# Another hand-written order for the opening of a fused window-attention and squared-ReLU kernel

## The chip, the core and the metric

The kernel runs on one core of a Trainium2 chip. The metric is device time in microseconds (us) of one execution, as the median of several runs. The core has five engines that run side by side and meet through semaphores: PE (matrix products, with PEld as its weight loads), DVE (vector), ACT (activation functions), POOL (GpSimd, which here also issues most of the loads) and SP (which issues the other loads and the stores). Each engine executes its own instructions strictly in the order in which the program issued them.

## The reference

Four batches of 768 tokens, 8 heads of 64. A token attends to the 128 latest tokens and to the first 4 ("sinks"). The attention output, 3072 x 512, goes through two dense layers with a squared ReLU between them.

```python
scores = scale * np.matmul(q, k.transpose(0, 1, 3, 2))
keep = is_sink | in_window            # 4 sinks, window of 128
a = softmax(np.where(keep, scores, -1e9))
x = (a @ v).transpose(0, 2, 1, 3).reshape(B * S, H * D)
h = x @ w_in                          # 512 -> 2048
r = np.maximum(h, 0.0)
out = (r * r) @ w_out                 # 2048 -> 512
```

## The kernel before

Everything is cut into some 990 small steps ("ops"), each of which is a function that issues one or a few instructions on one engine. The steps are built by loops over batches, groups and pairs of heads, and numbered in the order of building. They are then issued in the order of a long string, `ORDER`, written into the file. A word of it is a step's number, sometimes with a letter for the engine (`p` PE, `d` DVE, `a` ACT, `g` POOL; the first engine that the step allows otherwise) and with `+0` or `+1` for the PSUM pool that it takes a buffer from. PSUM is held as four buffers of two banks, two in a pool `den` and two in a pool `att`; SBUF scratch is handed out from pools of numbered buffers (`qr`, `qs`, `expm`, `r` and others) in the same way. A buffer is taken from the front of a list of free ones, so the order also settles which earlier step a later one has to wait for. `DUMMIES` says ahead of which steps `warm` issues passes of PE whose result is overwritten: 128x128 products with the identity, into the buffer that the step is about to fill.

```python
            o.engine = names[word[-1]] if word[-1] in names else next(iter(o.engines))
            for s in o.takes:
                if len(s.pools) > 1:
                    s.pool = s.pools[int(chosen.pop(0))]
                s.room = free[s.pool].pop(0)
            self.idle = DUMMIES.get(n, 0)
            o.run(o.engine)
```

Batch 0 is taken in three groups of 256 tokens. The first two groups are loaded as float32 with SP and ACT queues (steps 7 to 15), cast on DVE or ACT, turned on PE, copied out of PSUM, and so on; the third is loaded by POOL with a cast on the way (27 to 30). The steps that the prediction names are these:

| steps | what they do |
|---|---|
| 7, 9 / 8, 10 | load keys / queries of group 0, head pairs 0-1 and 2-3 |
| 12, 14 / 13, 15 | the same for group 1 |
| 19, 20, 22, 23, 31, 32 | load value tiles 0 to 5 (POOL) |
| 21, 24, 25, 26 / 33 to 36 | load the four quarters of the first / second weight matrix (POOL) |
| 27, 28 / 29, 30 | load keys / queries of group 2; 37 to 44 those of batch 1 |
| 991 | passes that warm PE up |
| 55, 60 / 56, 61 | cast keys / queries of group 0; 88, 93 / 89, 94 those of group 1 |
| 57, 62 | turn (transpose) group 0, pairs 0-1 and 2-3: the first two turns; 58, 59, 63, 64 copy them out |
| 90, 95 | the same for group 1; 91, 92, 96, 97 copy them out |
| 67, 68, 75, 76 | scores of group 0 (the mask is added by a product with `ident`); 69, 70, 77, 78 their exponentials |
| 71, 73, 79, 81 | weighted values of group 0; 72, 74, 80, 82 divide by the sums |
| 83, 85 | turn the attention output of group 0; 84, 86 copy it out |
| 100, 101, 110, 111 | scores of group 1; 102, 104, 112, 114 exponentials; 103, 105, 113, 115 masks |
| 66, 98, 99 | sink keys, sink scores, sink exponentials |
| 106, 108, 116, 118 | values of group 1; 107, 109, 117, 119 divide; 120 to 123 turn and copy out |
| 152 to 183 | first dense layer of groups 0 and 1: two PE steps, a ReLU and a square for each of 8 blocks |
| 124 to 151 | turn, scores, values of group 2 |
| 282 to 289 | second dense layer of group 0 |
| 331, 332, 334 / 278, 279 | sums of the first / second weight matrix, used later by products that save a multiplication |
| 184 | the PE step next after 289, the last word that the change touches |

All loads that POOL issues go through one queue, in the order of issue. From step 184 on the order is the same in both kernels, to the end of the program.

Of the kernel before, what the change touches and what calls it, by code (L numbers as in the profile page):

```python
# [18 lines left out]


ORDER = """
990 1 0 2 7 8 9 10 11 12 13 14 15 16 17 18 56a 991+0 55d 61a 3 60d 57+1 62+0 19 20 59a 5 6 58d 4 65 63d 67+0 21 64a
75+1 69 89d 22 77 23 76+0 68+0 24 25 70 71+1 88d 73 93d 90+0 78 79+1 72 94a 81 74 83+0 92d 100+1 91a 80 102 82 95+0 66
97d 26 85 110+1 101+1 96d 103g 104 84d 98+0 27 86d 152+0 105g 99 112 111+0 153 114 115g 106+1 113d 28 29 116+1 108
160+0 107 117 154a 30 109 118 119 161 120+1 121a 31 122 168+1 123d 169 32 33 34 155a 170a 162d 172+1 331 164+0 176+0
171d 163a 165 35 166d 36 167d 156+1 173 157 177 174d 124+1 158a 37 38 125a 126d 39 180+1 127+0 332 133+1 181 129d 178a
128a 136 130+1 179d 282+1 182d 334 131 141+1 132+0 140+1 183d 283 40 144 142 137g 284 285 41 145d 159d 143d 134 146+1
135d 147 286 138+1 287 288 278 139 42 43 148+0 175a 150 149d 151d 289 44 279 184+1 290 185 193+0 280 281 200+0 201 291
194 45 204+1 196+0 202 46 203 205 198a 186 197 207a 293 206 187+0 199a 216+0+0 47 48 195a 217 49 188d 234+1+0 50 235
190+0 219 208+0 87 292 237 209 295 191 218 297+0 189 220 51 336 52 212 53 210a 294 211 255+0 252+1 254 299 298 256 54  # L30
253a 257 444 223+0+1 333 238d 445 192a 226 304 213 224 221+0 312 222 300 241+1+0 301 214+0 296 244 215 302 225 446
# [26 lines left out]
985 967d 969 983 984 989 986 988 987  # L58
"""
DUMMIES = {  # L60
    57: 31, 62: 24, 75: 4, 85: 3, 110: 4, 991: 29,
}


# [1345 lines left out]
```

## Time and profile before

| | us |
|---|---|
| runs | 211.52, 211.09, 210.98; median 211.09 |
| the profiled execution's own time | 209.94 |
| its span, first to last instruction | 208.2 |
| PE busy | 200.9 (96%) |
| DVE busy | 178.0 (85%) |
| ACT busy | 131.6 (63%) |
| POOL busy | 98.6 (47%) |

In the rows that the prediction shows, a row of the timeline is: start, duration, engine, line of the program, operation, tile written <- tiles read, shape, how many in a row; in brackets the idle time ahead of it and what ended that. L503 is a turn, L609 and L602 are scores, L678 values, L727 the turn of the attention output, L762 the first dense layer, L990 the second dense layer of group 0, L185 and L1372 the passes that are thrown away; L192 and L194 are copies and casts on ACT and DVE, L630 an exponential, L642 and L218 masks on DVE and POOL, L694 and L695 the division, L776 and L778 the ReLU. A matmul's end is modelled and some 0.2 us after the next one starts, so the cost of a step on PE is read from one start to the next. A row of the windows has the window, its length, the busy time of PE, PEld, DVE, ACT and POOL in it, the granted clock of PE, and two numbers on the loads.

### The profile page before, as it was taken

The numbers are of one execution on the slowest core, as the hardware profiler recorded it, in microseconds if no ns is written. First come the engines' busy times: TensorE is split into PE (matmuls) and PEld (weight loads), VectorE is DVE, ScalarE is ACT, GpSimd is POOL, SyncE is SP. The second block draws the span as 40 slices with busy tenths as digits, with TensorE's granted clock in tenths as the row PEclk, the third lists the DMA queues.
The fourth block names the chain that finished last, engine by engine and source line by source line (L and its number), as shares of the span: only waits on it lengthen the run. The fifth ranks groups of instructions, "written<-read, shape, count | busy, mean of one in ns | idle before, by whom it ended". The sixth has DMA issues, their size and how long they took to land.

```text
span 208.2 us, 6087 instructions
## 1 busy us (share of the span) xinstructions
PE 200.9 (96%) x2535; PEld 177.6 (85%) x2535; DVE 178.0 (85%) x343; ACT 131.6 (63%) x205; POOL 98.6 (47%) x141
## 2 busy tenths in 40 slices
PE   7979999999899999999999999999999999999993
PEld 7757997579878889889878988998889999999893
DVE  5385767989999998999998888999989998998853
ACT  2678428718988168899888448989871452584010
POOL 7767983899489936989523529000280000000000
PEclk9999999999999999999999999999999999999999
DMA  5999999999999999999999995901023220200205
GB/s 162 218 216 202 184 186 213 177 155 179 148 61 118 156 137 241 92 188 154 129 138 229 108 136 152 159 0 25 4 50 127 57 82 22 101 0 3 99 5 201
DMA packets 96043, 26.12 MB, mean 125 GB/s; under 512 B 86800, under 2 KB 93456, under 8 KB 96016
## 3 DMA queue, kind: packets, MB, share of 16 engines
q0 software_dynamic: 69248, 12.59, 82.7%
q1 hardware_dynamic: 25568, 12.49, 28.6%
q10 hardware_dynamic: 1200, 0.66, 1.1%
q8 instruction: 20, 0.33, 0.6%
q14 instruction: 7, 0.06, 0.1%
HBM read 27.30 MB, written 6.29 MB: 161 GB/s over the span
## 4 chain that ended last, share of the span: by engine, by line
PE 76%; DVE 10%; DMA 6%; ACT 5%; issue 1%; ACTq 0%
PE py L1239 25%; PE pm L892 25%; PE pm L762 9%; DMA qr<-in_q_dram 6%; PE po L678 5%; PE ps L609 4%; PE py L990 3%; PE py L1100 2%; PE pt L503 1%; DVE sg L1213 1%; DVE xn_sb L695 1%; DVE r L942 1%; ACT gT_sb L915 1%; ACT qkT L192 1%; DVE gT_sb L1213 1%
## 5 line engine op out<-in xcount | busy, mean ns | idle before, releaser
L630 ACT ACTIVATE expm<-ps 128x1024 bf16<-128x1024 f32 (+1 forms) x48 | 44.1, 953 | 10.0 <-PE ps L609 8.9
L218 POOL TENSOR_SCALAR_AFFINE_SELECT expm<-expm 128x512 bf16<-128x512 bf16 x38 | 26.5, 730 | 46.9 <-ACT expm L630 21.5
L942 DVE CUSTOM_DVE_ANT_0 r<-pm,t 128x512 bf16<-128x512 f32 x54 | 36.0, 684 | 1.6 <-PE pm L892 1.2
L1239 PEld LDWEIGHTS <-gT_sb 128*128 128x128 bf16 x320 | 30.4, 98 | 4.5 <-issue 0.9
L892 PEld LDWEIGHTS <-w_in_sb 128*128 128x128 bf16 x384 | 32.5, 114 | 1.7 <-issue 1.5
L192 ACT ACTIVATE t<-pm 128x512 f32<-128x512 f32 x42 | 24.7, 600 | 13.4 <-PE pm L892 12.7
L192 ACT ACTIVATE osb<-py 128x256 f32<-128x256 f32 (+1 forms) x36 | 14.0, 397 | 19.9 <-PE py L1239 15.0
L892 PEld LDWEIGHTS <-wi 128*128 128x128 bf16 x288 | 24.7, 114 | 0.8 <-issue 0.7
L1239 PEld LDWEIGHTS <-sg 128*128 128x128 bf16 x240 | 22.5, 98 | 3.1 <-DVE sg L1213 0.3
L762 PE MATMUL pm<-xT,w_in_sb 128*128 128x256 bf16 x192 | 22.7, 273 | 0.4 <-DVE xT L194 0.4
L892 PE MATMUL pm<-xs,wi 128*128 128x256 bf16 (+1 forms) x192 | 21.6, 246 | 0.0
L892 PE MATMUL pm<-xs,w_in_sb 128*128 128x256 bf16 (+1 forms) x192 | 21.5, 246 | 0.0
L762 PEld LDWEIGHTS <-w_in_sb 128*128 128x128 bf16 x192 | 20.5, 114 | 1.1 <-issue 0.8
L1239 PE MATMUL py<-wt,gT_sb 128*128 128x256 bf16 x160 | 20.7, 273 | 0.2
L1239 PE MATMUL py<-wt,sg 128*128 128x256 bf16 x160 | 20.8, 273 | 0.0
L1239 PE MATMUL py<-w_out_sb,gT_sb 128*128 128x256 bf16 x160 | 20.4, 273 | 0.0
L915 ACT ACTIVATE gT_sb<-r 128x1024 bf16<-128x1024 bf16 x17 | 18.0, 1057 | 1.8 <-DVE r L942 1.6
L678 PE MATMUL po<-v,expm 128*128 128x65 bf16 x352 | 18.0, 193 | 0.5 <-ACT expm L630 0.3
L678 PEld LDWEIGHTS <-expm 128*128 128x128 bf16 x352 | 16.8, 97 | 1.8 <-ACT expm L630 0.5
L695 DVE TENSOR_TENSOR xn_sb<-po,rc 128x512 bf16<-128x512 f32 (+1 forms) x28 | 17.2, 615 | 1.0
L1253 DVE TENSOR_TENSOR osb<-py,osb 128x256 f32<-128x256 f32 x30 | 12.1, 415 | 4.7 <-PE py L1239 4.6
L609 PE MATMUL ps<-qkT 64*128 64x128 bf16 (+1 forms) x256 | 14.5, 238 | 0.9 <-ACT expm L630 0.6
(108 smaller groups left out, 382.2 us busy)
## 6 DMA issues: line engine op xcount, KB each, us to landing
out_dram<-osb SPq DMA_DIRECT2D x11, 512.0 KB, 3.4
v<-in_v_dram POOLq DMA_DIRECT2D x24, 128.0 KB, 6.3
qn<-in_k_dram POOLq DMA_DIRECT2D x20, 128.0 KB, 6.6
qn<-in_q_dram POOLq DMA_DIRECT2D x20, 128.0 KB, 6.2
w_in_sb<-in_moe_w_in_dram POOLq DMA_DIRECT2D x4, 512.0 KB, 9.4
w_out_sb<-in_moe_w_out_dram POOLq DMA_DIRECT2D x4, 512.0 KB, 10.0
qr<-in_k_dram SPq DMA_DIRECT2D x4, 256.0 KB, 6.8
qr<-in_q_dram ACTq DMA_DIRECT2D x2, 256.0 KB, 4.1
```

Of the source, the lines that this page charges most:

```text
L192: return nc.scalar.activation(out=dst, in_=src, func=AF.Copy)
L218: nc.gpsimd.affine_select(out=e_tile, in_=e_tile, compare_op=ALU.is_ge, fill=fill, base=i - 1, pattern=[[0, n], [1 if i else -1, 128]], ch ...
L609: nc.tensor.matmul(ps[:, h2, o:o + w], lhsT=qkT_sb[r, m, 1, c, :], rhs=qkT_sb[r, m, 0, qb:qb + w // 128, :], start=(i == 0 and not biased) ...
L630: nc.scalar.activation(out=x[:, :, o:512], in_=bank_t["s", b, s, m][:, :, o:512], func=AF.Exp, scale=scale)
L678: touch(("po", b, s, m0), e, nc.tensor.matmul(pv[:, i, h2, :], lhsT=lhsT, rhs=rhs, start=(n_ == 0), stop=(n_ == len(mms) - 1)), j)
L695: touch(("po", b, s, m0), e, nc.vector.tensor_tensor(out=xn_sb[:, 2 * s:2 * s + 2, 128 * (m0 + j0):128 * (m0 + j0 + nj)].rearrange("p i (j ...
L762: nc.tensor.matmul(pm[:, i, :], lhsT=w_in_sb[:, fb // 4, kb, fb % 4:512:4], rhs=xT[:, c0 // 256:(c0 + cw) // 256, kb, :], start=(kb == 0), ...
L892: touch(tag, e, nc.tensor.matmul(y[:, bk, i, :], lhsT=weights(name, f0 + i, a), rhs=rhs[:, a, :], start=fresh and i == 0 and a == 0, stop= ...
L915: nc.scalar.activation(out=d, in_=x, func=AF.Square)
L942: touch(tag, e, nc.vector._custom_dve(TENSOR_ADD_SAT, out=d.rearrange("p n c -> p (n c)"), in0=T["y"][:, 1].rearrange("p n c -> p (n c)"), ...
L1239: touch((b, u), e, nc.tensor.matmul(region(name), lhsT=x[:, i, :], rhs=w_[:, i, :], start=first and i == 0, stop=i == HB - 1, skip_group_c ...
L1253: ins = nc.vector.tensor_tensor(out=d, in0=region(of), in1=d, op=ALU.add)
```

## The change

The first 188 words of `ORDER` hold the same steps in another order (the first 16 stand as they were), with another engine for 25 of them and the other PSUM pool for 19. SP and ACT issue the same loads in the same order. POOL issues its loads in the same order too, with less between them: 27 stands ahead of mask 103 instead of behind it, masks 105, 115 and 137 go from POOL to DVE, and mask 135 comes from DVE to POOL, between 43 and 44. The dummy passes go from 31 to 9 ahead of step 57, from 24 to 14 ahead of 62; those ahead of 75 (4), 85 (3) and 110 (4) go, and 7 ahead of 95 and 3 ahead of 83 are new. The 29 of step 991 stay.

```diff
@@ -19,13 +19,13 @@
 ORDER = """
-990 1 0 2 7 8 9 10 11 12 13 14 15 16 17 18 56a 991+0 55d 61a 3 60d 57+1 62+0 19 20 59a 5 6 58d 4 65 63d 67+0 21 64a
-75+1 69 89d 22 77 23 76+0 68+0 24 25 70 71+1 88d 73 93d 90+0 78 79+1 72 94a 81 74 83+0 92d 100+1 91a 80 102 82 95+0 66
-97d 26 85 110+1 101+1 96d 103g 104 84d 98+0 27 86d 152+0 105g 99 112 111+0 153 114 115g 106+1 113d 28 29 116+1 108
-160+0 107 117 154a 30 109 118 119 161 120+1 121a 31 122 168+1 123d 169 32 33 34 155a 170a 162d 172+1 331 164+0 176+0
-171d 163a 165 35 166d 36 167d 156+1 173 157 177 174d 124+1 158a 37 38 125a 126d 39 180+1 127+0 332 133+1 181 129d 178a
-128a 136 130+1 179d 282+1 182d 334 131 141+1 132+0 140+1 183d 283 40 144 142 137g 284 285 41 145d 159d 143d 134 146+1
-135d 147 286 138+1 287 288 278 139 42 43 148+0 175a 150 149d 151d 289 44 279 184+1 290 185 193+0 280 281 200+0 201 291
+990 1 0 2 7 8 9 10 11 12 13 14 15 16 17 18 56d 60a 55d 991+0 3 19 57+0 61d 20 5 6 4 62+1 65 59a 67+0 58a 21 64d 89d
+63a 68+0 75+1 88d 69 70 76+1 22 71+0 77 23 72 73 78 24 94a 79+1 90+0 93d 92a 95+1 80 91d 81 96a 74 100+0 82 101+0 25
+26 102 83+1 97d 66 84d 27 104 85 110+1 111+0 103g 86d 152+1 112 28 113d 105d 98+0 99 153 106+0 108 114 115d 154a 116+1
+118 29 160+1 109 161 162a 107 30 119 117 120+0 31 155d 163a 122 121d 123d 32 168+0 156+1 331 33 172+0 157 169 164+1
+170a 165 34 35 158d 173 166a 124+1 125a 127+0 36 159d 176+1 129a 177 126d 174a 140+1 133+1 37 128d 171d 142 136 180+1
+181 282+0 38 178d 167d 137d 132+0 141+1 182a 130+0 39 283 40 144 143d 41 134 42 43 332 284 285 131 145d 146+0 175a 147
+135g 278 179a 286 138+1 139 287 288 148+0 150 334 151d 44 149a 279 183d 289 184+1 290 185 193+0 280 281 200+0 201 291
...
 DUMMIES = {
-    57: 31, 62: 24, 75: 4, 85: 3, 110: 4, 991: 29,
+    57: 9, 62: 14, 95: 7, 83: 3, 991: 29,
 }
```

## The prediction

> **What bounds the kernel now.** I read the page first, then windows over the opening, then the chain of waits, then the timelines of PE, ACT and DVE there.
>
> ```profile
> span 208.2 us, 6087 instructions
> PE 200.9 (96%) x2535; PEld 177.6 (85%) x2535; DVE 178.0 (85%) x343; ACT 131.6 (63%) x205; POOL 98.6 (47%) x141
> PE 76%; DVE 10%; DMA 6%; ACT 5%; issue 1%; ACTq 0%
> ```
> ```profile
> 10.40:15.60 5.20, 3.86 (x63) 2.74 (x63) 4.22 (x13) 3.76 (x6) 3.56 (x5) 1.00 1.51 216
> 20.80:26.00 5.20, 5.20 (x66) 5.18 (x63) 3.92 (x10) 2.58 (x4) 5.20 (x7) 1.00 1.72 184
> ```
>
> PE is the bound: three quarters of the chain are its own work, and from 20.8 us it has no hole in the window. It has holes in the opening (3.86 of 5.20 us from 10.4 on), and some of its work there is dummy passes. So the change can gain only by bringing PE sooner to step 184, the first that both kernels order alike; whatever it gains or loses there then moves the rest, which is PE's, by as much.
>
> What sets the pace in the opening is in the chain:
>
> ```profile
> 4.95 8.88 DMA qr<-in_q_dram
> ...
> 13.91 0.63 ACT qs L192
> ...
> 15.49 1.29 DVE qkT L194 x2
> 16.78 0.67 DVE xT L194 x2
> ...
> 17.50 1.03 PE pm L762 x8
> ```
>
> The load of the second half of group 1's queries (15) lands at 13.83; ACT casts it (94), PE turns it (95), DVE copies, and the first dense layer starts at 17.50 (step 152). The first two turns, with the most dummy passes, are not on it at all.
>
> **Part 1: the dummies and the first scores.**
>
> ```profile
> 1.27 3.27 PE L1372 MATMUL pw<-tri 128*128 128x128 bf16 x29 [1.27 <-DVE tri L224]
> 4.34 2.01 PE L185 MATMUL pt<-ident 128*128 128x128 bf16 x31
> 6.18 0.61 PE L503 MATMUL pt<-ident,qs 128*128 128x128 bf16 x8
> 6.63 1.50 PE L185 MATMUL pt<-ident 128*128 128x128 bf16 x24
> 7.97 0.61 PE L503 MATMUL pt<-ident,qs 128*128 128x128 bf16 x8
> 10.73 0.50 PE L602 MATMUL ps<-sg,ident 128*128 128x384 bf16 x2
> 11.44 0.63 PE L678 MATMUL po<-v,expm 128*128 128x65 bf16 x6
> L380 POOL DMA_DIRECT2D v<-in_v_dram x2: 882/967/1052, 1.9 to 2.9; - x2
> DMA to landing us min/median/max: 6.8/7.8/8.8
> 6.14 0.43 DVE L194 CAST qs<-qr 128x512 bf16<-128x512 f32 x1 [1.01 <-DMA qr<-in_k_dram]
> 6.83 0.63 ACT L192 ACTIVATE qs<-qr 128x512 bf16<-128x512 f32 x1 [1.25 <-DMA qr<-in_q_dram]
> ```
>
> A dummy pass costs (7.97 - 6.63) / 24 = 0.056 us. Turn 57 now needs both casts on DVE: queries at 4.95 (when they land), keys behind, 0.43 to 0.63 each by the two cast rows, so about 6.1; before it stood behind the dummies until 6.18. Turn 62 needs cast 61, now on DVE: 6.83 + 0.43 = 7.26, and the 14 dummies behind turn 57 (6.1 + 0.44 + 14 x 0.056 = 7.3) end just then; so 7.3 against 7.97. The four scores at 0.70 each, without the 4 dummies between them (0.23), end at 7.3 + 0.44 + 4 x 0.70 = 10.6 against 11.44. That is 0.85 us sooner, and it is the gain that the edit shows. I count it as nothing: the values behind them (71) read value tile 1, issued at 2.93 and landed 8.8 later, at 11.74. In the profile PE starts 71 at 11.44 and its 6 passes still take 0.63, waiting in the middle for that tile. No load ahead of it moves in any queue, so 71 ends at 11.9 in both. If that cover were gone, 0.85 us would be the price.
>
> **Part 2: from the values to the first dense layer.** 73, 79 and turn 90 follow without a wait: the last score ends at 10.6, and an exponential takes 1.02 at most (the full-width one below), so all are done by 11.7. Three steps (some 0.2 for each of the values, 0.45 for the turn, as 57 took) bring PE to 12.7, and the 7 dummies of 95 to 13.1. Then PE waits for cast 94, as before.
>
> ```profile
> 14.92 1.02 ACT L630 ACTIVATE expm<-ps 128x1024 bf16<-128x1024 f32 x1
> 16.96 1.02 ACT L630 ACTIVATE expm<-ps 128x1024 bf16<-128x1024 f32 x1 [0.71 <-PE ps L609]
> 18.15 1.95 ACT L630 ACTIVATE expm<-ps 128x1024 bf16<-128x1024 f32 x2
> 15.49 1.29 DVE L194 COPY qkT<-pt 128x512 bf16<-128x512 bf16 x2 [0.36 <-PE pt L503]
> 16.70 0.74 DVE L194 COPY xT<-px 128x512 bf16<-128x512 bf16 x2
> L695 DVE TENSOR_TENSOR xn_sb<-po,rc 128x256 bf16<-128x256 f32 x8 | 3.4, 424 | 0.3
> ```
>
> 95 goes at 14.59 instead of 15.07 (it no longer waits for a buffer that a copy on ACT frees), but now values 81 stand behind it: 15.03, ended 15.38; division 82 on DVE 15.42 to 16.06 (0.18 + 0.42 and the step between). Turn 83 takes the buffer that 82 frees, so it and its 3 dummies wait: 16.10, 16.27, ended 16.66. Copy 84 at 16.70, 86 0.33 behind it, ended 17.44: step 152 at 17.5. Before: 17.50. The chain comes out at the same place, by other steps. So removing the 3 + 4 dummies of 85 and 110 is worth nothing, and the 3 of 83 cost under 0.1.
>
> ACT pays for it: copy 92 now waits behind cast 94 on ACT (14.5), and copy 96 behind turn 95 (15.24, some 0.5), so exponential 102 starts at 15.75 instead of 14.92. ACT had a hole of 0.71 ahead of 104, which takes most of that: 102 15.75, sink keys 16.65, 104 17.0 (before 16.96), 112 17.9, sinks 18.8, 114 19.1 (before 18.15 + 0.9, the second of the pair).
>
> **Part 3: to the end of the reordered part.**
>
> ```profile
> L642 DVE TENSOR_TENSOR expm<-expm,tri 128x1024 bf16<-128x1024 bf16 x4 | 2.7, 682 | 1.8 <-ACT expm L630 1.8
> 20.78 1.04 PE L762 MATMUL pm<-xT,w_in_sb 128*128 128x256 bf16 x8
> 22.02 1.04 PE L762 MATMUL pm<-xT,w_in_sb 128*128 128x256 bf16 x8
> 23.34 8.90 PE L762 MATMUL pm<-xT,w_in_sb 128*128 128x256 bf16 x80
> 33.94 0.39 PE L609 MATMUL ps<-qkT 64*128 64x128 bf16 x6
> 34.26 1.06 PE L762 MATMUL pm<-xT,w_in_sb 128*128 128x256 bf16 x8
> 36.45 0.84 PE L609 MATMUL ps<-qkT 64*128 64x128 bf16 x18
> 37.22 2.76 PE L990 MATMUL py<-w_out_sb,gT_sb 128*128 128x512 bf16 x12
> 45.31 3.66 PE L762 MATMUL pm<-xT,w_in_sb 128*128 128x256 bf16 x32
> ```
>
> Masks 105 and 115 leave POOL for DVE (0.68 each). DVE does 113 first, at 18.97 when 112 ends, then 105, ended 20.25. PE, through 152, 98, 153 and 106, is ready for values 108 at 19.95 and waits until 20.29: +0.34, a hole that was not there. 116 and 118 follow (115 ends 20.85), and block 160 starts at 21.4. In the profile it starts at 20.78 with 118 still to come behind it; the next start but one, 22.02, less the half-block of 0.87 (80 passes in 8.90, its last 0.2 overlapping), puts 118 at 0.37. So the change stands at 21.4 where the kernel before stands at 21.15: +0.25, all of it from that hole.
>
> From here both have the same PE work left. What differs is how often PE goes between full-height products and scores of 64 rows: six passes alone take 0.32 (33.94 to 34.26), eighteen together 0.77 (36.45 to 37.22), so each change costs some 0.1. Scores 140 and 133 now stand together, 132, 141 and the sinks too, and 98 takes the place of 111: three changes fewer, -0.3 (0 if they are not the cause). I find no new wait on the way: the ReLUs that move to ACT (162, 166, 174, 182) end 0.1 to 0.5 ahead of the steps that take their buffers; those that move to DVE (158, 178) over 1 us ahead; turn copies 121 and 123, on DVE behind square 155, end at 24.45, and step 156 goes at 24.5, 0.04 late. Step 184 comes at 45.31 + 0.25 - 0.3 = 45.3, as before.
>
> **POOL and DVE at the end.** POOL issues 27 and 28 about 3.3 us sooner. That lands nothing sooner:
>
> ```profile
> L371 POOL DMA_DIRECT2D qn<-in_k_dram x2: 893/901/909, 17.2 to 21.3; - x2
> DMA to landing us min/median/max: 5.9/7.4/9.0
> ```
>
> Issued 4.1 us apart they land 1.0 apart (26.2 and 27.2), so the queue ahead of them sets it. Loads 41 to 43 are the same case, and the queue's order is kept. On DVE 334 and square 183 now stand ahead of the weight sums at 45 to 49, which end some 0.4 later; the copies behind them start late by that much, and PE has a half-block of 1.75 to do before it needs them, so I cost it at nothing, and at 0.4 without that cover.
>
> **The sum**: scores -0.85, taken back by value tile 1 (+0.85); 152 at 17.5 (0.0); hole at 108 +0.34, of which +0.25 is left at 160; changes of height -0.3; the rest 0. On the profiled execution's own 209.94 us (1.7 outside its span) that is 210.0. The median of the runs stands 1.15 above it, so 211.1. Bounds of what the trace doesn't show: the opening's part from -0.85 (nothing holds PE) to +0.83 (all of 102's delay goes through).
>
> **The rivals.** *Faster: the loads come sooner than the same row says.* If PE isn't held at 11.74 and 13.83, the 0.85 us survives: 210.2. For it: PE really is ready sooner. Against: no issue ahead of either load moves, on any queue. It decides when tile 1 lands before 11.0 and the queries of step 15 before 13.0.
>
> *Slower: ACT's late start goes through.* The line 102, 104, 112, 113, 105, 108 has no slack left in it; each tenth that ACT or DVE loses there is a tenth for PE. If the whole 0.83 of 102 goes through to 160: 211.9. Against it speaks the hole of 0.71 ahead of 104.
>
> [...] The 29 passes of 991 take some 0.106 each (3.27, less the 0.3 of the last, over 28), those behind them 0.056: PE begins at half rate. [...]
>
> **How the numbers follow.** 0.3% (0.63 us) is about what a measurement can tell from no change. No change 0.5; loads sooner 0.23 (210.2); ACT's delay 0.17 (211.9); clock 0.1 (212.5). So faster 0.23, same 0.5, slower 0.27, and the time is that of the likeliest, 211.1. The no-change case alone spans 210.6 to 211.7; the range, 210.0 to 212.1, takes in the faster case and ACT's, and leaves out the clock's.
>
> **What would show it.** Right: first score near 7.8 us, values 71 still with a wait in the middle and ended near 11.9; cast 94 still at 13.9; 152 within 0.2 of 17.5; a hole of some 0.3 us on PE ahead of values near 20; step 184 within 0.4 of 45.3; granted clock 1.00 from 5 us on. Wrong: 71 ended well before 11.7, a window under clock 1.00 in the first 20 us, or a wait on PE between 21 and 45 us.

## The result, and the profile after

The changed kernel takes 209.44 us (median; 209.20 to 209.73), the kernel before 211.12 in the same comparison (210.98 to 211.52). The ratio is 0.9918, with a 95% interval of 0.9898 to 0.9938: 1.7 us faster, where 211.1 and no change were forecast and 210.0 was the low end of the range. Two further comparisons of the two programs gave 0.9924 (0.9896 to 0.9953) and 0.9936 (0.9908 to 0.9963). Three of the highest times in the tables below (213.06 and 214.18 us of the kernel before, 216.44 of after_late17) are executions in a slower state and don't count in the ratios.

The profiled execution of the changed kernel took 209.26 us. The head of its page, and the chain of waits by engine:

```profile
span 207.6 us, 6021 instructions
PE 199.6 (96%) x2500; PEld 176.2 (85%) x2502; DVE 174.7 (84%) x342; ACT 133.9 (64%) x208; POOL 96.2 (46%) x137
...
PE 80%; DVE 6%; ACT 6%; DMA 4%; issue 2%; POOL 0%; ACTq 0%; POOLq 0%; DVEq 0%
```

PE is busy for 1.3 us less, with 33 passes fewer in `DUMMIES`, and is the bound as before. The windows over the opening:

```profile
10.40:15.60 5.20, 3.49 (x66) 2.71 (x66) 4.26 (x13) 3.60 (x6) 4.73 (x6) 1.00 1.49 218
20.80:26.00 5.20, 5.20 (x56) 5.19 (x53) 3.14 (x11) 2.08 (x2) 1.45 (x3) 1.00 1.70 185
```

PE has more room between 10.4 and 15.6 us than before (3.49 busy against 3.86) and still has no hole from 20.8 on. PE's own rows in the timeline:

```profile
4.34 1.17 PE L185 MATMUL pt<-ident 128*128 128x128 bf16 x9
6.00 0.62 PE L503 MATMUL pt<-ident,qs 128*128 128x128 bf16 x8 [0.49 <-DVE qs L194]
6.46 0.94 PE L185 MATMUL pt<-ident 128*128 128x128 bf16 x14
7.24 0.74 PE L503 MATMUL pt<-ident,qs 128*128 128x128 bf16 x8
7.81 0.49 PE L602 MATMUL ps<-sg,ident 128*128 128x384 bf16 x2
...
10.61 0.23 PE L678 MATMUL po<-v,expm 128*128 128x65 bf16 x2
11.91 0.64 PE L678 MATMUL po<-v,expm 128*128 128x65 bf16 x16 [1.07 <-DMA v<-in_v_dram]
...
13.26 0.62 PE L503 MATMUL pt<-ident,qs 128*128 128x128 bf16 x8
...
16.91 1.03 PE L762 MATMUL pm<-xT,w_in_sb 128*128 128x256 bf16 x8
...
19.34 0.20 PE L678 MATMUL po<-vs,es 128*128 128x65 bf16 x1
19.61 0.24 PE L678 MATMUL po<-v,expm 128*128 128x65 bf16 x2
...
44.63 3.66 PE L762 MATMUL pm<-xT,w_in_sb 128*128 128x256 bf16 x32
```

The scores end 0.83 us sooner (values start at 10.61, not 11.44), and the values then wait 1.07 us for value tile 1: both as forecast. But step 152 stands at 16.91 instead of 17.50 and step 184 at 44.63 instead of 45.31. On ACT:

```profile
12.62 0.63 ACT L192 ACTIVATE qs<-qr 128x512 bf16<-128x512 f32 x1 [1.08 <-DMA qr<-in_q_dram]
...
14.85 1.02 ACT L630 ACTIVATE expm<-ps 128x1024 bf16<-128x1024 f32 x1 [0.33 <-PE ps L609]
```

Cast 94 waits for the queries of step 15 and starts at 12.62; in the first profile of the kernel before, on which the forecast rested, it started at 13.91. So 0.68 us of the gain is seen between these two profiles. The rest is not: the first profile of before took 209.94 us, and the median of its executions 211.1, while the changed kernel's profile and median agree within 0.2 us. Where an ordinary execution of the kernel before loses that microsecond, and why the changed one doesn't, is what the experiments are about.

### The profile page after: what moved, and what is told of

Its sections match the earlier page's. It is cut to its first block, busy times and chain, and to the rows that moved or that the text cites. A ratio compares the mean times of both kernels' runs of the same rounds, so it can differ in the third digit from the quotient of the medians.

```text
span 207.6 us, 6021 instructions
## 1 busy us (share of the span) xinstructions
PE 199.6 (96%) x2500; PEld 176.2 (85%) x2502; DVE 174.7 (84%) x342; ACT 133.9 (64%) x208; POOL 96.2 (46%) x137
## 4 chain that ended last, share of the span: by engine, by line
PE 80%; DVE 6%; ACT 6%; DMA 4%; issue 2%; POOL 0%; ACTq 0%; POOLq 0%; DVEq 0%
PE py L1239 28%; PE pm L892 25%; PE pm L762 9%; PE po L678 6%; PE ps L609 4%; DMA v<-in_v_dram 4%; PE py L990 3%; ACT expm L630 2%; PE py L1100 2%; PE pt L503 1%; DVE r L942 1%; ACT gT_sb L915 1%; PE px L727 1%; DVE xn_sb L695 1%; ACT qkT L192 1%
## 5 line engine op out<-in xcount | busy, mean ns | idle before, releaser
L218 POOL TENSOR_SCALAR_AFFINE_SELECT expm<-expm 128x512 bf16<-128x512 bf16 x34 | 24.0, 740 | 42.2 <-DVE xn_sb L695 19.5
L1239 PE MATMUL py<-wt,sg 128*128 128x256 bf16 x160 | 20.8, 273 | 0.0
```

The costliest lines, as they stand in the source:

```text
L218: nc.gpsimd.affine_select(out=e_tile, in_=e_tile, compare_op=ALU.is_ge, fill=fill, base=i - 1, pattern=[[0, n], [1 if i else -1, 128]], ch ...
L1239: touch((b, u), e, nc.tensor.matmul(region(name), lhsT=x[:, i, :], rhs=w_[:, i, :], start=first and i == 0, stop=i == HB - 1, skip_group_c ...
```

## The experiments

Each kernel of the first, second, fourth and fifth group was timed in some 6 to 12 executions beside the kernel before on the same chip; times are medians with lowest and highest. The third group is single profiled executions.

### Which part of the change does it

```diff
 dummies_only: the old ORDER, and
-    57: 31, 62: 24, 75: 4, 85: 3, 110: 4, 991: 29,
+    57: 9, 62: 14, 95: 7, 83: 3, 991: 29,
 order_only: the new ORDER, and the old line of DUMMIES
 b_again, a_again: the two kernels unchanged
```

> The kernel before once more, unchanged, to see how its profiled execution stands to its own runs (209.94 against a median of 211.1) and whether the load of group 1's second queries (step 15), which landed at 13.82 us in the first profile and at 12.53 us in that of the change, lands at the same time again. Theory 'load' (the landing of step 15 sets the first dense layer's start, and the order itself is worth little): in a usual run of before step 15 lands at 13.8 us or later, and step 152 starts at 17.5 us or later; a profile near 211 us shows it near 15. Theory 'order' (the new order itself saves PE time): step 15 lands within 0.3 us of 12.5 to 13.8 us in every profile, and the 1.2 us between profile and median is elsewhere, behind 152. Theory 'clock' (before's usual runs lose a stretch at half the granted clock): spans near 209.4 us come with a mean granted clock under 1.000, by some 0.006 for each 1.2 us.

> The changed kernel once more, on the same chip as the others of this call, for intervals against them. All theories: 0.992 of before, within 0.002, spans near 207.6 us. Theory 'load' expects its profile to have step 15 landed near 12.5 us again and step 152 started near 16.9 us; if step 15 lands near 13.8 us instead, step 152 starts near 17.5 us and the span is near 208.2 us.

> The order of before with the dummy passes of the change (9 ahead of 57, 14 ahead of 62, 7 ahead of 95, 3 ahead of 83, none ahead of 75, 85 and 110). Theory 'order': 0 to -0.3 us against before, ratio 0.999 to 1.001, since the values 71 wait for value tile 1 at 11.74 us and step 152 for copy 86. Theory 'dummies' (fewer passes ahead of the first two turns are the gain): ratio 0.992 to 0.995. [...]

> The order of the change with the dummy passes of before (31 ahead of 57, 24 ahead of 62, 4 ahead of 75, 3 ahead of 85, 4 ahead of 110). Theory 'order': ratio 0.992 to 0.994, the whole gain, since the dummies end before value tile 1 lands at 11.8 us. Theory 'dummies': ratio 0.998 to 1.001. Theory 'load': as the landing of step 15 in its profile has it, 152 some 4.4 us behind that landing.

| kernel | us | ratio to before (95%) |
|---|---|---|
| before, all its runs beside these | 211.08 (209.84 to 212.97) | |
| b_again | 210.92 (209.70 to 212.06) | 0.9983 (0.9957 to 1.0010) |
| a_again | 209.68 (209.44 to 210.36) | 0.9924 (0.9896 to 0.9953) |
| dummies_only | 209.98 (209.54 to 210.42) | 0.9935 (0.9910 to 0.9961) |
| order_only | 210.09 (209.24 to 212.03) | 0.9971 (0.9938 to 1.0005) |

The numbers of passes alone bring most of it; the order alone brings nothing that is clear of no change (its interval ends at 1.0005). The spread is as telling as the median: with 31 and 24 passes ahead of the first two turns a kernel's executions lie over 2.4 to 3.1 us, with 9 and 14 over 0.9. order_only reaches the lowest time of the four, and has single executions at 212.

### Which passes, and more and fewer of them

```diff
 two_turns, against before:
-    57: 31, 62: 24, 75: 4, 85: 3, 110: 4, 991: 29,
+    57: 9, 62: 14, 75: 4, 85: 3, 110: 4, 991: 29,
 more_passes, against before:
+    57: 53, 62: 34, 75: 4, 85: 3, 110: 4, 991: 29,
 no_turn_passes, against after:
+    95: 7, 83: 3, 991: 29,
 late_load, against after: SP issues load 15 behind the next load of sink values
```

> The kernel before with only the passes ahead of the first two turns cut (9 ahead of 57, 14 ahead of 62; the 4, 3 and 4 ahead of 75, 85 and 110 stay, none ahead of 95 and 83). Theory 'passes': these two groups are what costs a microsecond in most executions, since PE begins at half rate and the moment at which it goes to full rate differs (4.4 to 6.4 us in six profiles), so that 31 and 24 passes hold the turns for longer in one execution than in another. It expects 209.7 to 210.2 us (0.993 to 0.996 of before), all runs below 211, and step 152 at 17.4 to 17.7 as in the kernel with all of the new counts. Rival 'small groups': the passes ahead of 75, 85, 110 (or those ahead of 95 and 83) are the gain: 210.7 to 211.2.

> The kernel before with 22 more passes ahead of turn 57 (53) and 10 more ahead of 62 (34), as many as the change removes. Theory 'passes': 32 x 0.056 = 1.8 us later at the first scores with an early rise, up to 0.8 more with a late one; the value tile that lands near 11.8 hides little of it since the scores of before end near there already. 1.0 to 2.0 us slower than before: 212.1 to 213.1 (1.005 to 1.010), with a spread as wide as that of before. Rival 'hidden': scores are not what sets step 152, the passes before them cost nothing: 211.1 (1.000).

> The changed kernel with no passes ahead of turns 57 and 62 (7 ahead of 95, 3 ahead of 83 and the 29 of the start stay). Theory 'passes': what is left of them (9 and 14) holds nothing for long, so 209.3 to 209.7 us (0.991 to 0.993), as the changed kernel. [...]

> The changed kernel with the load of the second half of group 1's queries (15) issued behind the next small load of sink values on SP's queue, so that it lands later by the time that this one's issue takes (2 us in the profiles). Theory 'landing': the prediction's step at 17.5 rested on a landing at 13.82, which only the first profile shows; where it lands by 12.7, the new order has cast 94 at 12.6 and step 152 at 16.9 to 17.1. With a landing at 13.8 or later, 152 goes to landing + 3.7, at 17.4 or later, and the time to 210.0 to 210.7 (0.995 to 0.998). Rival 'no link': ACT's and DVE's own work sets 152 in the new order: 152 stays within 0.15 of 17.0 and the time at 209.4 to 209.7.

| kernel | us | ratio to before (95%) |
|---|---|---|
| before, beside these | 210.98 (209.78 to 213.06) | |
| two_turns | 209.82 (209.12 to 210.26) | 0.9922 (0.9892 to 0.9952) |
| more_passes | 212.25 (211.17 to 212.73) | 1.0051 (1.0025 to 1.0077) |
| no_turn_passes | 209.95 (209.19 to 211.23) | 0.9957 (0.9930 to 0.9983) |
| late_load | 209.89 (209.20 to 211.62) | 0.9952 (0.9924 to 0.9981) |

two_turns settles the place: cutting the 22 + 10 passes ahead of steps 57 and 62 brings the whole of that gain, and the small groups are worth nothing that shows. It keeps the old order, and its ratio (0.9922) can't be told from the changed kernel's (0.9924), so nothing here shows that the new order is worth anything beside the passes. And yet its profile has no gain in the opening at all:

```profile
11.96 0.46 PE L678 MATMUL po<-v,expm 128*128 128x65 bf16 x10 [0.76 <-DMA v<-in_v_dram]
...
17.49 0.71 PE L762 MATMUL pm<-xT,w_in_sb 128*128 128x256 bf16 x5 [0.29 <-DVE xT L194]
```

Value tile 1 takes back what the scores gained, and step 152 stands at 17.49, as in the first profile of before: what the prediction said of these passes is what happens in these two executions. So the microsecond that the cut saves in the median had to be looked for in other executions of the kernel before.

more_passes costs 1.27 us for 32 passes (1.8 us of them at 0.056), with half the spread of before (1.6 against 3.3): that contradicts the expectation, which had the spread come from the passes and stay as wide. no_turn_passes goes the other way: in its profile the sixteen products of both turns together, with PE resting ahead of them, are slow,

```profile
6.30 1.89 PE L503 MATMUL pt<-ident,qs 128*128 128x128 bf16 x16 [1.76 <-DVE qs L194]
```

(the changed kernel takes 0.62 for eight), and the full rate comes only at 9.7 us. Step 184 stands at 44.85 all the same, within the 44.63 to 45.11 of the changed kernel's profiles, and 0.9957 (0.9930 to 0.9983) overlaps with its ratio. So whether the 9 and 14 passes are worth keeping is not shown. late_load could not tell what it was made for: the queries were issued 0.7 us later and landed at 12.58 all the same, and its 0.2 us over the changed kernel are within the spread.

### Looking at more executions of the kernel before

No edit: b_look1 to b_look3 are the kernel before, o_look is order_only.

> The kernel before, unchanged, one more profiled execution, to see where the microsecond lies that most of its executions take over the first profiled one (209.94). Theory 'passes': 57 starts at 6.18 + 0.48 x (rise of the clock - 4.56) us, the first score 2.23 behind it, and step 152 at 17.5 or at the first score + 8.6, whichever is later; at 45 us the execution stands as far behind the first profile as at 152. Rival 'late stalls': the opening is the same within 0.25 us whatever the rise is, and what is over 209.94 is lost behind 45 us, in waits for transposing loads and stores that land late (0.78 near 131 us in one profile).

> The same kernel and question as in the look before. Theory 'passes': the part over 209.94 us lies ahead of 45 us and goes with the first score (152 at the first score + 8.6 where that is later than 17.5). Rival 'late stalls': it lies behind 45 us, in single waits of 0.2 to 0.9 us for DMA.

> The same kernel and question as in the two looks before, with the same numbers: 'passes' puts what is over 209.94 us ahead of 45 us, 'late stalls' behind it.

> The new order with the old numbers of passes, one more profiled execution; its times fell in two groups, 209.2 to 210.5 and 211.2 to 212.0. Theory 'passes': an execution of the upper group has its clock rise past 7 us, turn 57 past 7.4 and 152 past 18.0; one of the lower group has 57 at 6.18 + 0.48 x (rise - 4.56) and 152 at 17.4 or before. Rival 'late stalls': 152 at 17.4 in both groups, and the difference behind 45 us.

In the table, "184" is the start of that step, "opening" its distance from 45.31 (the first profile of before), and "late" what is left of the span's distance from 208.24 us, that is, what is lost or won behind step 184.

| profile | its time | first score | 184 | opening | late |
|---|---|---|---|---|---|
| before, first | 209.94 | 8.41 | 45.31 | 0 | 0 |
| b_again | 211.04 | 9.05 | 45.54 | +0.23 | +0.79 |
| b_look1 | 212.53 | 8.10 | 45.59 | +0.28 | +2.21 |
| b_look2 | 210.38 | 8.67 | 45.65 | +0.34 | +0.02 |
| b_look3 | 211.71 | 9.19 | 45.68 | +0.37 | +1.40 |
| order_only | 209.72 | 9.21 | 45.11 | -0.20 | 0 |
| o_look | 211.19 | 9.54 | 45.80 | +0.49 | +0.67 |
| dummies_only | 210.07 | 8.07 | 45.42 | +0.11 | 0 |
| two_turns | 210.26 | 7.94 | 45.34 | +0.03 | +0.29 |
| after | 209.26 | 7.81 | 44.63 | -0.68 | 0 |
| a_again | 209.70 | 7.87 | 44.82 | -0.49 | +0.25 |

Both theories have a part, and the larger one is "late stalls". In the opening, "first score + 8.6" gives 17.79 for b_look3 (17.83 measured), and in b_look1 (the queries of step 15) and b_look2 (value tile 1, landed at 12.64) a late load sets 152 instead. The opening's part comes from PE's rate. It starts at about half rate (0.106 us a pass against 0.056 later) and goes over at a moment that differs from execution to execution. The 31 passes and the turn behind them in b_look1 and in o_look:

```profile
4.14 1.89 PE L185 MATMUL pt<-ident 128*128 128x128 bf16 x31
5.87 0.61 PE L503 MATMUL pt<-ident,qs 128*128 128x128 bf16 x8
```
```profile
4.34 3.13 PE L185 MATMUL pt<-ident 128*128 128x128 bf16 x31
7.31 0.61 PE L503 MATMUL pt<-ident,qs 128*128 128x128 bf16 x8
```

The same passes take 1.89 and 3.13 us (2.01 in the first profile of before), and the first turn starts at 5.87 or 7.31. The step from 0.106 to 0.056 us a pass came at 3.91 us in the one and 6.92 in the other. The second feeder of the opening is a load: in b_look1, with the earliest rise of all, the queries of step 15 landed at 14.10 and put step 152 at 17.78.

The larger part is lost 70 us behind the changed code. b_look1 there (PE and ACT in the timeline):

```profile
115.92 0.66 ACT L192 ACTIVATE osb<-py 128x256 f32<-128x256 f32 x2 [1.54 <-DMA out_dram<-osb]
116.35 1.03 PE L1239 MATMUL py<-wt,sg 128*128 128x256 bf16 x8 [0.91 <-ACT osb L192]
...
132.34 0.40 PE L568 MATMUL pk<-qkT,kblk 128*32 128x512 bf16 x4 [1.08 <-DMA qkT<-qn]
```

At 116 us ACT waits 1.54 for a store to free its output buffer, and PE 0.91 for ACT; at 132 PE waits 1.08 for a transposing load. b_look3 has the first (1.05 on PE), b_again the second (0.78), o_look the second (0.64 for that load). The changed kernel at the same two places:

```profile
115.38 0.39 ACT L192 ACTIVATE osb<-py 128x256 f32<-128x256 f32 x1 [0.25 <-PE py L1239]
...
129.17 0.40 PE L568 MATMUL pk<-qkT,kblk 128*32 128x512 bf16 x4
```

No wait for DMA at either. All twenty profiles can be set side by side in this way, since PE's work from step 184 on is the same in each but for the delays put in below. Its distance from the first profile of before stays the same within 0.1 us, except for jumps near 72, 114, 120 and 129 us of that profile and one near 198 (0.41 us, in no_turn_passes). The losses over 0.5 us all lie near 114 and 129, which are the two places just shown.

### Giving the time back behind the opening

Four of the five profiles that stood 0.2 to 0.5 us late at step 184 had such a wait, and none of the other profiles so far lost over 0.3 us at these two places. But being late doesn't decide it: b_look1 and b_look2 are one program, stand at +0.28 and +0.34, and lose 2.21 and 0.02. If being late has a part in it, a delay put in behind the opening must bring the waits back.

```diff
 after_late9, _late17, _late30: the changed kernel with   + 200: 9  /  17  /  30
 before_late17: the kernel before with                     + 200: 17
```

> The changed kernel with 9 passes added ahead of step 200, the turn behind 184 (48.1 us), where PE has no hole: everything from there on comes 9 x 0.056 = 0.5 us later, the opening stays. Theory 'offset': waits of 0.7 to 1.2 us for transposing loads and stores near 117 and 131 us come only where the compute stands 0.2 to 0.5 us behind the first profile of before at 45 us (four of five such profiles had one, none of the nine others). The changed kernel stands 0.3 to 0.7 ahead, and with the passes 0.2 ahead to 0.2 behind: 210.0 to 210.4 us, little above its own time and 0.5. Rival 'sum': the passes cost their own 0.5 and nothing else: 210.0 to 210.3.

> The same with 17 passes (0.95 us), so that the changed kernel stands 0.2 to 0.6 behind the first profile of before from 49 us on, as before's usual execution does. Theory 'offset': the late waits come with it: 211.0 to 211.7 us (0.999 to 1.003 of before), with single executions past 212, and a profile with a wait of 0.5 us or more near 117 or 131. Rival 'sum': 210.4 to 210.8 us, spread of 1 us as in the changed kernel.

> The same with 30 passes (1.7 us), so that it stands 1.0 to 1.4 behind. Theory 'offset' as a band, as the kernel with more passes hints (1.76 behind, late waits of 0.4 in all): 211.3 to 211.8 us. As a threshold: every execution has the waits: 212.0 to 213.0. Rival 'sum': 211.2 to 211.5.

> The kernel before with the same 17 passes (0.95 us) ahead of step 200, so that it stands 0.9 to 1.5 behind its first profile. Theory 'offset' as a band: it leaves the band, and its late waits go: 211.0 to 211.6 us, at most 0.5 over before, with a narrower spread. Rival 'sum', and 'offset' as a threshold: 211.9 to 212.2 us, with the spread of before.

The first three are set against the 209.68 us of the changed kernel in an earlier comparison, the last against the kernel before in the first row.

| kernel | delay | us | over the kernel without it | ratio to before (95%) |
|---|---|---|---|---|
| before, beside these | | 211.01 (210.26 to 214.18) | | |
| after_late9 | 0.50 | 211.11 (210.32 to 212.31) | 1.4 | 1.0014 (0.9993 to 1.0035) |
| after_late17 | 0.95 | 212.21 (210.94 to 216.44) | 2.5 | 1.0062 (1.0027 to 1.0097) |
| after_late30 | 1.7 | 213.33 (212.80 to 214.40) | 3.7 | 1.0117 (1.0090 to 1.0143) |
| before_late17 | 0.95 | 211.35 (210.84 to 213.30) | 0.3 | 1.0023 (1.0001 to 1.0046) |

"Sum" falls on both sides: half a microsecond that touches nothing ahead of 48 us cost 1.4, and 0.95 cost 0.3 in the other kernel. In after_late9, whose opening is that of the changed kernel to 0.01 us, nearly the whole excess is one wait:

```profile
131.01 0.40 PE L568 MATMUL pk<-qkT,kblk 128*32 128x512 bf16 x4 [1.49 <-DMA qkT<-qn]
```

The kernel before, moved by 0.95, has ten of its twelve executions under 211.8, so in the median it pays less than the delay, as the band said. But its profile is of one of the other two (212.99) and shows that the store's wait can come there too; PE waits 1.0 for this row:

```profile
117.59 0.66 ACT L192 ACTIVATE osb<-py 128x256 f32<-128x256 f32 x2 [1.52 <-DMA out_dram<-osb]
```

The band's numbers fall as well: after_late9 should have stayed in the free zone (0.2 ahead to 0.2 behind) and did not, and after_late30 did not come out of it again.

The load that PE waits for near 131 us shows what differs. It took 2.4 us from issue to landing in eleven of the twenty profiles and 3.2 to 4.5 in nine, and its issue doesn't tell which: a_again and after_late9 both issued it at 126.46 and had it at 128.88 and at 130.87. It was slow in none of the seven undelayed profiles with 14 passes or fewer ahead of each turn, in four of the eight with 24 or more, and in all five with a delay at 48 us. So the slow landings go with the passes and with the delay; by what way is not shown.

In after_late17 and after_late30 a second thing shows. The turns of the opening, which the added passes come 40 us behind, ran at half rate (14 passes from 7.11 to 8.61 in after_late17, 0.107 us each):

```profile
7.11 1.70 PE L185 MATMUL pt<-ident 128*128 128x128 bf16 x14
8.61 1.06 PE L503 MATMUL pt<-ident,qs 128*128 128x128 bf16 x8
```

The full rate came at 10.65 and 10.13 us, and step 184 at 45.66 and 45.70, a microsecond later than in the changed kernel's profile. Executions like these owe a microsecond to the opening and not to the delay, so of the three kernels after_late9 is the clean one.

### The same in the old order, and the changed kernel once more

```diff
 two_turns_late9, against two_turns:
-    57: 9, 62: 14, 75: 4, 85: 3, 110: 4, 991: 29,
+    57: 9, 62: 14, 75: 4, 85: 3, 110: 4, 991: 29, 200: 9,
 after_third: the changed kernel unchanged
```

> The kernel before with only the passes of the first two turns cut (which took 209.82 us), and 9 passes added ahead of step 200 at 48 us, 0.5 us that PE can't hide. Theory 'offset': the cut had gained 1.1 us since it lets the compute meet the loads of 100 to 131 us some tenths sooner; given back behind the opening, the waits come back with them: 210.8 to 211.3 us as before (0.998 to 1.002), single executions past 211.7. Rival 'opening': what the passes disturb lies in the first 15 us, and the delay adds its own 0.5 alone: 210.2 to 210.5 us, none past 211.

> The changed kernel, unchanged, beside the other one and once more beside before, since three kernels with passes behind the opening came out further over it than either theory gave, two of them with the clock's rise past 10 us. If that late rise belongs to the changed kernel's own opening (its PE rests between the passes of the start and the first turn), some executions lie 1 us or more over the rest, at 210.5 or more; if not, all stand at 209.2 to 210.4 as in the two calls before.

| kernel | us | ratio to before (95%) |
|---|---|---|
| before, beside these | 210.75 (209.97 to 212.86) | |
| two_turns_late9 | 211.28 (210.61 to 212.51) | 1.0006 (0.9974 to 1.0038) |
| after_third | 209.65 (209.06 to 210.54) | 0.9936 (0.9908 to 0.9963) |

With the 0.5 us given back at 48 us the cut of the passes is worth nothing any more: 1.46 us over two_turns (which was timed in another comparison; the ratio goes from 0.9922 to 1.0006), three times the delay, and all twelve executions above 210.6. Its profile, one of the quicker executions (210.93), has the wait at the same instruction, 0.34 us long:

```profile
130.84 0.40 PE L568 MATMUL pk<-qkT,kblk 128*32 128x512 bf16 x4 [0.34 <-DMA qkT<-qn]
```

So a delay that disturbs nothing ahead of 48 us takes back the whole gain of the cut, and two thirds of that are more than the delay itself. That fits passes which act mainly by how late they leave the stretch from 100 to 131 us. It isn't proof that the passes of the opening act in this way: the profiles show a part in the opening too, and this delay is itself nine more passes. after_third has step 184 at 45.11 (0.20 ahead) and loses 0.10 behind it, in 209.84 us; its rate rose at 5.08. Its highest execution, 210.54, leaves room for a late rise now and then, but none of the three profiles of the unchanged program shows one.

## Why the prediction was wrong

**The step that failed most: "The median of the runs stands 1.15 above it".** The sum was made for one execution and the distance to the median added as a constant. That distance is made of things that this change moves. Over the five profiles of the kernel before, the opening stands 0.24 us behind the first one and 0.88 is lost in late waits, 1.1 together, about the 1.15 of the prediction. Over the three of the changed kernel (after, a_again, after_third) the same two are -0.46 and +0.12. The difference, 0.70 in the opening and 0.77 in late waits, is 1.5 us, beside 1.1 to 1.7 between the medians of the three comparisons. These are means over five and three executions, so the split is rough; that both parts exist is shown by the table, and that time put in behind the opening can cost more than itself by the delays. Why the changed kernel has so few of the late waits stays open. (The sum itself is 209.9, not 210.0: 209.94 - 0.05. Nothing hangs on it.)

**"152 at 17.5 (0.0)": mis-sized.** This is the part in the opening. It stood at 16.91, 17.10 and 17.39 in the three profiles, and 184 0.20 to 0.68 ahead of 45.31. The anchor was the landing of step 15's queries at 13.82. Of the five profiles of before two have it that late (13.82, 14.10), three at 12.42 to 13.29, and the changed kernel has it at 12.47 to 12.66. The view showed one execution's landing, and it was taken for the load's time. (In all ten profiles in the new order it landed at 12.44 to 12.68, so the order may have a part in that; no run separates it.) The old order makes nothing of an early landing (b_again: landed at 12.62, 152 at 17.68; two_turns, with early scores too: 12.99 and 17.49); the new order seems to. That an early landing is what puts 152 sooner in the new order is argued from these rows: late_load, made to test it, did not delay the landing. The rest of the walk holds as a sum: from 152 to 184 the sum has -0.05 (+0.25 and -0.3), and the three profiles have -0.09.

**"ACT pays", 102 at 15.75:** it came at 14.85, with cast 94 ahead of it 1.3 sooner. With the cast at 13.91 the walk might have held; no run tried it.

**Scores -0.85, hidden by value tile 1: right as far as 71.** -0.83, with a wait of 1.07 in the middle of 71, and in two_turns the gain is taken back in full. "If that cover were gone" was the wrong worry, though: the cover hides the passes only when the rate rises early. In b_look3, with turn 57 at 6.96 instead of 6.18 and the first score 0.78 later than in the first profile, 152 stood at 17.83.

**A late rise of PE's rate has no term in the sum.** Turn 57 shows what it moves in the kernel before, with 31 passes ahead of it: it lies between 5.87 and 6.96 in its profiles, and at 7.31 with the same passes in o_look, beside 6.00 to 6.24 in the three profiles of the changed kernel. Nor does value tile 1 always hide it: with the rise at 10.65 in after_late17 the values start at 12.78 instead of 10.61, 2.2 later, and step 184 1.0 later. In the trace that the prediction read, the rise lies at 4.56, 3.3 us after the first pass; in the nine profiles with 31 or 53 passes ahead of turn 57, where PE had no rest, it lies between 3.91 and 6.92.

**The hole ahead of values 108: right** in place and near in size. The rows at 19.34 and 19.61 show it: 0.27 us from one start to the next, where 0.03 is usual between such rows, so 0.24 beside 0.34. The changes of height (-0.3) were not tested by themselves.

**The rivals.** "The loads come sooner" (210.2) had the right sign and half of the mechanism: the queries came before 13.0, value tile 1 did not come before 11.0. Neither of the slower times came. ACT's start went the other way: 102 was not late. The chances also carry 212.5 for the clock with 0.1, and no profiled run shows a drop of the rate in the opening: the granted clock reads 1.00 in every window of the changed kernel's first 20.8 us, step 152 takes 1.03 to 1.07 us in all twenty profiles, and in after_late9, where PE rests for 1.39 us between the rise and the first turn, the turn's eight products take 0.62. None of the rivals had an event behind step 184, since the order is the same there; that an unchanged stretch also takes the same time was assumed, and the late waits refute it.

## What to carry to other kernels

A profile is one execution: where its own time lies a microsecond from the median, look at more executions before adding that difference as a constant, for it may be the very thing that the change moves. Behind the changed stretch, ask which loads and stores arrive with no slack: a delay there can cost more than itself (0.50 us cost 1.4 in after_late9), and a deliberate delay of known length is a cheap way to see it. Passes that keep PE busy should not be counted by their full-rate time, since ahead of the rise each takes nearly twice as long (0.106 against 0.056 us).

## What the runs showed of the hardware

- The start of full rate on PE lay anywhere from 3.91 to 6.92 us in seventeen of the twenty profiles, and at 9.72, 10.13 and 10.65 in the other three, which are among the eight in which PE rests ahead of the first turn. The granted clock of a window doesn't show it: it reads 1.00 from 0 to 5.2 us of the first profile of before, where the 29 passes of step 991 take 0.106 us each.
- A delay of 0.50 us at 48 us, where PE has no hole, cost 1.4 us in the new order (after_late9) and 1.5 in the old one (two_turns_late9); 0.95 us in the kernel before cost 0.3. The excess is in single waits near 116 and 131 us for a store and a transposing load on SP's queue. Why these land late in some executions and not in others is open: the load took 2.4 us or 3.2 to 4.5, also when issued at the same time, and no run separated it from the transfers of SP and POOL beside it.
- No kernel tried was shown to be faster than the changed one. Fewer passes still (no_turn_passes) and the cut alone (two_turns) came within 0.3 us of it.
